# A recurrence and a mixture of experts on one core: first gate parts in pairs, first scores in quarters, last product in halves

## The chip, the core and the metric

The kernel runs on one core of one Trainium2 chip. The metric is the device time of one execution in microseconds (us), median of several runs. Before the change it is 399.98 us (399.85 to 400.6 over 3 runs).

The engines are named as the profile names them: PE is TensorE's matmul row and PEld its weight loads, DVE is VectorE, ACT is ScalarE, POOL is GpSimd, SP is SyncE, whose queue issues most transfers. L583 is line 583 of the kernel before the change.

## The reference

Two parts follow each other. The first is a recurrence over 768 time steps for 4 batches and 8 heads of width 48, with a state of 48 by 48 for each head:

```python
cur = einsum('bhd,bhe->bhde', u * kt, vt)
y[:, :, t] = einsum('bhd,bhde->bhe', rt, state + cur)
state = w * state + einsum('bhd,bhe->bhde', kt, vt)
```

Its output becomes 3072 rows (tokens) of 384. The second part is a mixture of 16 experts in 4 groups of 4. A row picks the group with the largest of 4 group scores, then the expert with the largest of that group's 4 scores; its gate weight is the product of the two softmax values. Then

```python
h = maximum(x[rows] @ w1[expert], 0.0)      # 384 -> 1024
out[rows] = gate * (h @ w2[expert])          # 1024 -> 384
```

All of it is float32.

## The kernel before

**Recurrence.** The 3072 rows are 24 tiles of 128 time steps, four tiles (one for each batch) side by side in time. Within a tile the recurrence is solved in parallel: r is multiplied by powers of the decay w, k by their inverse, and scores k times r for all pairs of time steps are masked to earlier ones. The main loop runs 24 steps `s` (from L860). A step multiplies values with the masked scores of its tile (`values`, L583), prepares scores (`scores`, L536) and masks (`mask`, a predicated copy on VectorE, L543) for tile s+1, or from step `CLOSE` = 5 on for tile s+2, turns k and r of a later tile on TensorE (`turn`, L511; evacuated by ScalarE for k, L520, and by VectorE for r, L522), updates the state (`update`, L594; `carry`, L604 to L608) and adds the state's share of the next tile's output (`state`, L574). GpSimd multiplies r, k and u for the diagonal (`own`, L489 and L490) and scales k (`scaled`, L493); ScalarE and VectorE lay the diagonal into the mask tile `am` (`diagonal`, L561; `diagonal_here`, L554).

**Gates.** The output of a tile leaves PSUM by a ScalarE copy (`values_out`, L612) and is turned into rows (`rows_out`, L630, L634). For the gate scores, four small products for each tile give the parts of a quarter of the columns (`gate_parts`, L619), a ScalarE copy `lT` (L624) takes them out, and a second product adds the quarters (`gate_sum`, L644). In groups of four tiles the routing follows on VectorE (`route_1` to `route_4`), and GpSimd scatters the rows by expert (L230). Steps 3, 4 and 6 do two tiles' gate parts, step 5 one, from step 7 on one for each step. Parts of even tiles below 7 go to the PSUM bank MS, the others to TR. MS also holds the state's update, the gate sums, the prefix and the counts.

**Range flag.** If a decay lies outside a range, the kernel falls back to a slow path. The flag is computed in step 0: `out_of_range` (L752, L753) on VectorE, a product over partitions (`all_out_of_range`, L756) and `in_range` (L759); `go_on` (L762) in step 8. It is used after the experts' counts, by `judge` (L771).

**Start.** Ahead of the loop TensorE does empty transposes of the identity (`turn_nothing`, L422): 13 at first, 2 behind the product that spreads u (L425), and 2 and 4 ahead of the turns of tile 1. The scores of tile 0 are 8 products of 128 by 128 (L530), those of later tiles quarters of 64 wide (L536), each in two passes.

**Experts.** Two experts' first 128 rows are done ahead; then 16 slots follow, slot 1 first and slot 0 last, with row counts as in `SLOTS`. A slot is products up (`up`, L1104), a ReLU on ScalarE (L1109) and products down. Slots 0 and 1 go down with rows on partitions (`rows_down`, L238 to L250): 8 products of 384 columns (L240), a scaling by the gate on ScalarE (L244), and an indirect row write by GpSimd (L245). The other slots go down with columns on partitions (`down`, L1116), from a rearranged copy `w2p` (L1094), and are written by `finish` in blocks (L1128). Weights are fetched three slots ahead by SP (L135, L141).

**Order.** The order on every engine is the order of the calls in the program; semaphores are put in from the tiles' reads and writes, and accesses of two engines to one PSUM bank of a tile are kept apart. One queue's instruction that waits holds all behind it.

Of the kernel before, what the change touches and what calls it, by code (L numbers as in the profile page):

```python
# [9 lines left out]
FP32 = mybir.dt.float32  # L10
I32 = mybir.dt.int32
# [18 lines left out]
def kernel(  # L30
# [52 lines left out]
    def cst(shape, name, dtype=FP32):  # L83
        return const.tile(shape, dtype, name=name)
# [34 lines left out]
    tagA = [cst([P, 2], f"tagA_{i}") for i in range(4)]  # L119
    idA = [cst([P, 1], f"idA_{i}", I32) for i in range(4)]  # L120
    okA = [cst([P, 1], f"okA_{i}", I32) for i in range(4)]
    cnt_s = cst([P, GE], "cnt_s")
# [128 lines left out]

    def tokens(i, n, count):
        nc.vector.memset(idA[i][0:n], NOWHERE)
        nc.vector.tensor_scalar(
            out=tagA[i][0:n, 0:1].bitcast(I32), in0=tagA[i][0:n, 0:1].bitcast(I32), scalar1=2, scalar2=None,
            op0=OP.logical_shift_right,
        )
        nc.vector.tensor_scalar(out=okA[i][0:n], in0=prow[0:n], scalar1=count[0:n], scalar2=None, op0=OP.is_lt)
        nc.vector.copy_predicated(idA[i][0:n], okA[i][0:n], tagA[i][0:n, 0:1].bitcast(I32))

# [13 lines left out]
    with ExitStack() as rec:  # L274
# [3 lines left out]
        rows_ps = YB[:, :, 2 * P : 4 * P]  # L278
        lT_at = (MS[:, 0:P], TR[:, 0, :])

        spare_at = [0]
# [21 lines left out]
        pre_ps = MS[:, 400 : 400 + 4 * GE]  # L303
        cnt_ps = MS[:, 464 : 464 + GE]

        def scratch(shape, i):
# [67 lines left out]

        nc.vector.memset(y_ps, 0.0)
        nc.vector.memset(padded(rp[0]), 0.0)
        nc.vector.memset(padded(rp[NRP - 1]), 0.0)
# [47 lines left out]
        nc.tensor.matmul(u_ps_all, lhsT=ones[0:1, :], rhs=u_row, start=True, stop=True, skip_group_check=True)  # L425
        turn_nothing(2)
        gates_in()
# [96 lines left out]
        def scores(n):  # L524
            kT, rT = rkT.pop((n, "kT")), rkT[n, "rT"]
            for hc in range(HC):
                for e in range(2):
                    rows = slice(DP * e, DP * e + D)
                    if n == 0:
                        nc.tensor.matmul(  # L530
                            PA[:, e, P * hc : P * (hc + 1)], lhsT=kT[rows, hc, :], rhs=rT[rows, hc, :],
                            start=True, stop=True, skip_group_check=True,
                        )
                        continue
                    for z in range(2):
                        nc.tensor.matmul(  # L536
                            PA[64 * z : 64 * (z + 1), e, P * hc + 64 * z : P * (hc + 1)],
                            lhsT=kT[rows, hc, 64 * z : 64 * (z + 1)], rhs=rT[rows, hc, 64 * z : P],
                            start=True, stop=True, skip_group_check=True,
                        )  # L540
# [72 lines left out]

        def gate_parts(n):
            yT = yTs[n]
            lT_ps = lT_at[n % 2 if n < 7 else 1]
            for q in range(NQ):
                e, j = q // 2, q % 2
                nc.tensor.matmul(  # L619
                    lT_ps[32 * q : 32 * (q + 1), :], lhsT=gwp[:, 4 * j + e, :], rhs=yT[:, e, j, :],  # L620
                    start=True, stop=True, skip_group_check=True,
                )
            lT = mid[n] = pool.tile([P, P], FP32, tag="lT", bufs=3, name="lT")
            nc.scalar.copy(lT, lT_ps)  # L624

# [59 lines left out]
        def count(n):  # L685
            nc.tensor.matmul(cnt_ps, lhsT=ones, rhs=cum[:, n, :], start=True, stop=True, skip_group_check=True)

        def keys():
# [62 lines left out]
        def out_of_range():  # L751
            nc.vector.tensor_tensor(out=same, in0=wcol, in1=wraw, op=OP.not_equal)  # L752
            nc.vector.reduce_max(out=same[:, 0:1], in_=same, axis=AX)  # L753

        def all_out_of_range():
            nc.tensor.matmul(cnt_ps[:, 0:1], lhsT=ones, rhs=same[:, 0:1], start=True, stop=True, skip_group_check=True)  # L756

        def in_range():
            nc.vector.tensor_scalar(out=not_ok, in0=cnt_ps[:, 0:1], scalar1=0.5, scalar2=None, op0=OP.is_gt)  # L759

# [66 lines left out]
        scores(0)  # L827
        nc.vector.tensor_mul(WL, pw[:, :, P // 2], pw[:, :, P // 2])
        nc.scalar.copy(wl, WL)
        for t in am[2:4]:  # L830
            nc.scalar.copy(diagonals(t)[:, 0:HERE], spread(nothing.to_broadcast([P, P]), 1, HERE))
        mask(0)
        turn_nothing(2)
        turn(1, "rT")
        turn_nothing(4, TR)
        turn(1, "kT")
# [23 lines left out]
        for s in range(NT):  # L860
# [44 lines left out]
            if s > CLOSE:  # L905
                update(s)
            values_out(s)
            if s == 0:
                own_term(1)
                out_of_range()  # L910
            for n, e, hc in waiting:
                diagonal(n, e, hc, hc + 1)
            waiting.clear()
            if s <= CLOSE:
                scores(s + 1)
                update(s)
                if s == CLOSE:
                    sum_own(s + 3)
                mask(s + 1)
# [5 lines left out]
            if far < NT:  # L925
                turn(far, "kT")
                turn(far, "rT")
            if s == 0:
                all_out_of_range()
                in_range()  # L930
            if whole:
# [7 lines left out]
            for c in range(NB - 1):  # L939
                if s == first(c) + 1:  # L940
                    route_e(c)
            for n in {4: (0, 1), 5: (2, 3), 6: (4,), 7: (5, 6)}.get(s, (s - 1,) if s > 7 else ()):
                gate_sum(n)
            for c in range(NB - 1):
                if s == first(c) + 2:
                    route_p(c)
                    if c == 2:
                        count(12)
            for n in {3: (0, 1), 4: (2, 3), 5: (4,), 6: (5, 6)}.get(s, (s,) if s > 6 else ()):
                gate_parts(n)  # L950
            if s < CLOSE:
                own_term(far)
            for c in range(NB - 1):
# [4 lines left out]
                if s == first(c) + 2:  # L958
                    if c == 2:
                        key = keys()  # L960
                    route_3(c)
                if s == first(c) + (2 if c >= NB - 3 else 3):
# [16 lines left out]
            if s + 1 < NT:  # L979
                state(s + 1)  # L980
            if s == CLOSE - 1:
                turn(s + 3, "kT")
                turn(s + 3, "rT")
                own_term(s + 3)
            if whole:
                diagonal(far, 1)
            if s >= CLOSE and s + 4 < NT:
                sum_own(s + 4)
            if s == 8:
                go_on()  # L990
        for job in late:
# [24 lines left out]
    with ExitStack() as moe:  # L1016
# [55 lines left out]
        def columns(p):  # L1072
# [4 lines left out]
            if s < 2:  # L1077
                tokens(2 + s, SLOTS[s], cnt_s[:, s : s + 1])
                return
# [62 lines left out]
        for p in range(GE):  # L1142
# [10 lines left out]
            if order[p] < 2:  # L1153
                i = order[p]
                po = next_of(downs)
                yt = pool.tile([P, DM], FP32, tag="yd", name="yd")
                rows_down(hTs[p], held(p)[1], 2 + i, SLOTS[i], po, yt)
            else:
                down(p, 0)
# [280 lines left out]
```

## Time and profile before

| | |
|---|---|
| median of 3 runs | 399.98 us (399.85 to 400.6) |
| the profiled execution's own time | 402.09 us |
| its span, first to last instruction | 400.3 us |
| mean granted TensorE clock | 0.998 |
| PE busy in the span | 388.7 us (97%) |
| POOL, ACT, DVE busy | 201.0, 180.4, 153.4 us |
| moved by DMA | 81.80 MB, 204 GB/s over the span |
| recurrence (24 steps) | about 12 to 129 us |
| experts' slots | about 152 to 393 us |

The profile is one execution, about 2 us slower by its own time than the median of the runs; durations are taken from it. The timeline lists runs of alike instructions: start in us, duration, engine, line, operation, tiles (output <- inputs), shape, count, and in brackets the idle time of the engine ahead of it with what seems to have ended it. Ends of matmuls are modelled, so the weight loads (PEld) show better when TensorE goes on. A wait for several things is put down to the one that came last, which is not always the one that held.

### The profile page before, as it was taken

To read this page: it belongs to the slowest core of one execution; us is meant where nothing else is said; L and a number is where in the kernel's file an instruction comes from. 1 tells how busy PE (TensorE), PEld (TensorE's weight loads), DVE (VectorE), ACT (ScalarE), POOL (GpSimd) and SP (SyncE) were. 2 spreads that over 40 slices of the span, in tenths; PEclk is the share of its full clock that TensorE was granted. 3 is DMA by queue.
4 is the path that set the end of the run, shared out by engine and by line. 5 is a ranking of instruction groups with operands and counts; after the bars stand their busy time and mean duration, and the time that the engine had idled before them with its cause. 6 is when DMAs were issued, how large, how long until landed. Compare 5 with 4: busy or idle time off the path is not lost.

```text
span 400.3 us, 10467 instructions
## 1 busy us (share of the span) xinstructions
PE 388.7 (97%) x3963; PEld 361.9 (90%) x3963; DVE 153.4 (38%) x405; ACT 180.4 (45%) x429; POOL 201.0 (50%) x265
## 2 busy tenths in 40 slices
PE   8999999999999999999999999999999999999992
PEld 6787899999888977899999999999999999999981
DVE  7887988888867602101202112111121221211110
ACT  4665888888875211432433424424244244244210
POOL 7999956999842412105162351532624524523542
PEclk9999999999999999999999999999999999999999
DMA  8998999995965977999999999999989999981000
GB/s 159 160 174 159 197 208 221 212 195 147 264 200 123 308 193 212 233 275 258 232 258 243 228 250 266 224 253 284 200 240 259 255 247 268 233 236 28 27 18 27
DMA packets 123118, 81.80 MB, mean 204 GB/s; under 512 B 96863, under 2 KB 114289, under 8 KB 123061
## 3 DMA queue, kind: packets, MB, share of 16 engines
q1 hardware_dynamic: 116019, 71.12, 77.1%
q0 software_dynamic: 4752, 9.55, 8.1%
q8 instruction: 32, 0.52, 0.6%
q10 hardware_dynamic: 2290, 0.40, 0.5%
q14 instruction: 25, 0.20, 0.2%
HBM read 69.89 MB, written 11.67 MB: 204 GB/s over the span
## 4 chain that ended last, share of the span: by engine, by line
issue 46%; PE 29%; POOL 18%; SPq 3%; DVE 2%; DMA 1%; POOLq 1%; ACT 0%
POOL out_dram L1128 16%; PE YB L583 6%; PE PA L536 6%; SPq L323 3%; PE TR L511 3%; PE YB L574 2%; PE YB L630 2%; PE RW L511 2%; PE MS L594 2%; PE TR L619 2%; PE MS L644 1%; DMA vt<-in_v_dram 1%; POOL out_dram L245 1%; PE TR L793 1%; DVE am L543 1%
## 5 line engine op out<-in xcount | busy, mean ns | idle before, releaser
L1128 POOL DMA_INDIRECT out_dram<-yt,idn x93 | 90.4, 972 | 137.1 <-DVE yt L1126 107.0
L1076 DVE STREAM_TRANSPOSE xe<-xg 128x672 f32<-128x672 f32 (+2 forms) x16 | 12.7, 796 | 121.0 <-DMA xg<-x_sorted 88.7
L1116 PE MATMUL YB<-hT,w2p 128*128 128x208 f32 (+10 forms) x336 | 58.7, 328 | 0.0
L1116 PE MATMUL PA<-hT,w2p 128*128 128x208 f32 (+10 forms) x336 | 58.1, 326 | 0.0
L1116 PEld LDWEIGHTS YB<-hT,w2p 128*128 128x128 f32 x336 | 55.8, 190 | 0.0
L1116 PEld LDWEIGHTS PA<-hT,w2p 128*128 128x128 f32 x336 | 55.3, 190 | 0.0
L561 ACT ACTIVATE am<-ident,du 128x128 f32<-128x128 f32 x152 | 50.5, 398 | 0.0
L1125 DVE STREAM_TRANSPOSE yt<-yT 128x672 f32<-128x672 f32 (+1 forms) x14 | 11.8, 842 | 80.4 <-ACT yT L1119 80.4
L1094 ACT COPY w2p<-w 128x1024 f32<-128x1024 f32 x42 | 41.1, 1045 | 3.0 <-DMA w<-in_moe_w_dram 3.0
L543 DVE COPY_PREDICATED am<-later,PA 128x1024 f32<-128x1024 int32 x24 | 31.7, 1323 | 10.8 <-PE PA L536 6.1
L1104 PE MATMUL MS<-xe,w 128*128 128x208 f32 (+12 forms) x192 | 32.8, 320 | 0.0
L1104 PE MATMUL TR<-xe,w 128*128 128x208 f32 (+12 forms) x192 | 32.8, 320 | 0.0
L1104 PE MATMUL RW<-xe,w 128*128 128x208 f32 (+12 forms) x192 | 32.8, 320 | 0.0
L1104 PE MATMUL SB<-xe,w 128*128 128x208 f32 (+12 forms) x192 | 32.7, 320 | 0.0
L1104 PEld LDWEIGHTS SB<-xe,w 128*128 128x128 f32 x192 | 30.8, 190 | 0.6 <-issue 0.2
L1104 PEld LDWEIGHTS MS<-xe,w 128*128 128x128 f32 x192 | 30.7, 190 | 0.0
L1104 PEld LDWEIGHTS RW<-xe,w 128*128 128x128 f32 x192 | 30.7, 190 | 0.0
L1104 PEld LDWEIGHTS TR<-xe,w 128*128 128x128 f32 x192 | 30.7, 190 | 0.0
L230 POOL DMA_INDIRECT x_sorted<-xt,place_i x16 | 16.1, 1003 | 23.6 <-DVE end L719 11.8
L536 PE MATMUL PA<-rT,kT 48*64 48x128 f32 (+1 forms) x736 | 25.6, 255 | 0.5 <-issue 0.5
L583 PE MATMUL YB<-am,vt 128*48 128x128 f32 x384 | 25.9, 277 | 0.1
L490 POOL TENSOR_TENSOR dg<-dg,ub 128x384 f32<-128x384 f32 x24 | 24.1, 1003 | 1.9
(220 smaller groups left out, 560.1 us busy)
## 6 DMA issues: line engine op xcount, KB each, us to landing
w<-in_moe_w_dram SPq DMA_DIRECT2D x128, 384.0 KB, 9.5
vt<-in_v_dram SPq DMA_DIRECT2D x24, 192.0 KB, 4.5
rp<-in_r_dram SPq DMA_DIRECT2D x23, 192.0 KB, 4.3
kt<-in_k_dram SPq DMA_DIRECT2D x22, 192.0 KB, 5.2
xg<-x_sorted SPq DMA_DIRECT2D x36, 85.8 KB, 10.3
x_sorted<-zeros SPq DMA_DIRECT2D x4, 392.0 KB, 4.7
out_dram<-yt,idn POOLq DMA_INDIRECT x93, 7.5
xg<-x_sorted SPq DMA_DIRECT2D x20, 73.5 KB, 8.9
```

The lines of the kernel that those rows point to most:

```text
L230: ins = nc.gpsimd.indirect_dma_start(out=xs_dram, out_offset=bass.IndirectOffsetOnAxis(ap=place_i[:, i : i + 1], axis=0), in_=xt[:, i].rea ...
L490: nc.gpsimd.tensor_mul(dg, dg, ub)
L511: nc.tensor.transpose(ps[:, hc, :], two, ident)
L536: nc.tensor.matmul(PA[64 * z : 64 * (z + 1), e, P * hc + 64 * z : P * (hc + 1)], lhsT=kT[rows, hc, 64 * z : 64 * (z + 1)], rhs=rT[rows, hc ...
L543: nc.vector.copy_predicated(am[n % NAM], later.unsqueeze(1).unsqueeze(1).to_broadcast([P, 2, HC, P]).bitcast(I32), PA.rearrange("p e (h t) ...
L561: nc.scalar.mul(am[n % NAM][:, e, hc, :], ident, dus[n][:, i : i + 1])
L583: nc.tensor.matmul(y_at(e, hc), lhsT=vt[:, n % 2, 2 * hc + e, :], rhs=amn[:, e, hc, :], start=(n < 4 and hc < 2), stop=True, skip_group_ch ...
L1076: nc.vector.transpose(xe[:, :, 0:nb, :], xg[:, 0:nb, 0:QW].rearrange("p i (ko a) -> p ko i a", a=32))
L1094: nc.scalar.copy(o4[:, kk], v4[:, kk])
L1104: nc.tensor.matmul(ph[:, i, 0:n], lhsT=w1[:, ko, P * (f + i) : P * (f + i + 1)], rhs=xe[:, ko].rearrange("p i b -> p (i b)")[:, 0:n], star ...
L1116: nc.tensor.matmul(po[:, 0:n], lhsT=w2p[:, d, fo, :], rhs=hT[:, fo, 0:n], start=(fo == 0), stop=(fo == FO - 1))
L1128: ins = nc.gpsimd.indirect_dma_start(out=out_q, out_offset=bass.IndirectOffsetOnAxis(ap=idn[:, i : i + 1].bitcast(U32), axis=0), in_=yt[:, ...
```

## The change

- **Gate parts.** `gate_parts` takes a list of tiles, writes their parts side by side in TR and takes them out with one copy. Steps 3 and 4 call it, and in step 4 `gate_sum` ahead of it, behind the `state` product of the next tile. In step 5 gate parts come ahead of the sums.
- **Step 4.** The copy `values_out` stands behind the waiting diagonals. The second k turned in step 4 goes to PA in place of TR.
- **First scores.** Tile 0 is done in quarters as the others; a memset clears the unwritten quarter of PA ahead.
- **Start.** The 2, 2 and 4 empty transposes behind the first 13 are gone. The product `WL` and the copy `wl` stand behind the first mask.
- **Range flag.** `out_of_range` moves to the end of step 8 and writes its column into `cum`; the count product of step 14 takes that column too; `in_range` reads it there, `go_on` runs in step 17. The product of step 0 is gone.
- **Last product.** The slot that comes last (slot 0, 96 rows) goes down in two halves of 192 columns, each with its own scaling and row write; row numbers for half rows come from `tokens`.

```diff
+    idH = [cst([P, 1], f"idH_{z}", I32) for z in range(2)]
...
-    def tokens(i, n, count):
+    def half_down(hT, w2, i, n, z, po, yt):
+        cols = slice(DM // 2 * z, DM // 2 * (z + 1))
+        for fo in range(FO):
+            nc.tensor.matmul(
+                po[0:n, 0 : DM // 2], lhsT=hT[:, fo, 0:n], rhs=w2[:, fo, cols], start=(fo == 0), stop=(fo == FO - 1),
+                skip_group_check=True,
+            )
+        nc.scalar.mul(yt[0:n], po[0:n, 0 : DM // 2], tagA[i][0:n, 1:2])
+        ins = nc.gpsimd.indirect_dma_start(
+            out=out.rearrange("n (z w) -> (n z) w", z=2),
+            out_offset=bass.IndirectOffsetOnAxis(ap=idH[z][0:n].bitcast(U32), axis=0),
+            in_=yt[0:n], in_offset=None, bounds_check=2 * N - 1, oob_is_err=False,
+        )
...
+    def tokens(i, n, count, halves=False):
+        tag = tagA[i][0:n, 0:1].bitcast(I32)
+        nc.vector.tensor_scalar(out=okA[i][0:n], in0=prow[0:n], scalar1=count[0:n], scalar2=None, op0=OP.is_lt)
+        if halves:
+            for z in range(2):
+                nc.vector.memset(idH[z][0:n], NOWHERE)
+            nc.vector.tensor_scalar(out=tag, in0=tag, scalar1=1, scalar2=None, op0=OP.logical_shift_right)
+            nc.vector.copy_predicated(idH[0][0:n], okA[i][0:n], tag)
+            nc.vector.tensor_scalar(out=tag, in0=tag, scalar1=1, scalar2=None, op0=OP.bitwise_or)
+            nc.vector.copy_predicated(idH[1][0:n], okA[i][0:n], tag)
+            return
...
-        lT_at = (MS[:, 0:P], TR[:, 0, :])
...
+        lost_ps = MS[:, 464 + GE : 464 + GE + 1]
...
         nc.vector.memset(y_ps, 0.0)
+        nc.vector.memset(PA.rearrange("p e (h z t) -> p e h z t", z=2, t=64)[64:P, :, :, 0, :].rearrange("p e h t -> p (e h) t"), 0.0)
...
         nc.tensor.matmul(u_ps_all, lhsT=ones[0:1, :], rhs=u_row, start=True, stop=True, skip_group_check=True)
-        turn_nothing(2)
...
-                    if n == 0:
-                        nc.tensor.matmul(
-                            PA[:, e, P * hc : P * (hc + 1)], lhsT=kT[rows, hc, :], rhs=rT[rows, hc, :],
-                            start=True, stop=True, skip_group_check=True,
-                        )
-                        continue
...
+        def gate_parts(some):
+            for i, n in enumerate(some):
+                for q in range(NQ):
+                    e, j = q // 2, q % 2
+                    nc.tensor.matmul(
+                        TR[32 * q : 32 * (q + 1), i, :], lhsT=gwp[:, 4 * j + e, :], rhs=yTs[n][:, e, j, :],
+                        start=True, stop=True, skip_group_check=True,
+                    )
+            m = len(some)
+            lT = pool.tile([P, m, P], FP32, tag=f"lT{m}", bufs=3 - m, name="lT")
+            nc.scalar.copy(lT, TR[:, 0:m, :])
+            for i, n in enumerate(some):
+                mid[n] = lT[:, i, :]
...
+        def count_and_range(n):
+            both = cum[:, n : n + 2, :].rearrange("p i e -> p (i e)")[:, 0 : GE + 1]
+            nc.tensor.matmul(
+                MS[:, 464 : 464 + GE + 1], lhsT=ones, rhs=both, start=True, stop=True, skip_group_check=True
+            )
...
-            nc.vector.reduce_max(out=same[:, 0:1], in_=same, axis=AX)
+            nc.vector.reduce_max(out=cum[:, 13, 0:1], in_=same, axis=AX)
...
         scores(0)
-        nc.vector.tensor_mul(WL, pw[:, :, P // 2], pw[:, :, P // 2])
-        nc.scalar.copy(wl, WL)
...
         mask(0)
-        turn_nothing(2)
+        nc.vector.tensor_mul(WL, pw[:, :, P // 2], pw[:, :, P // 2])
+        nc.scalar.copy(wl, WL)
         turn(1, "rT")
-        turn_nothing(4, TR)
         turn(1, "kT")
...
-            values_out(s)
+            if s != CLOSE - 1:
+                values_out(s)
             if s == 0:
                 own_term(1)
-                out_of_range()
             for n, e, hc in waiting:
                 diagonal(n, e, hc, hc + 1)
             waiting.clear()
+            if s == CLOSE - 1:
+                values_out(s)
...
-            if s == 0:
-                all_out_of_range()
-                in_range()
...
+            summed = {4: (0, 1), 5: (2, 3), 6: (4,), 7: (5, 6)}.get(s, (s - 1,) if s > 7 else ())
+            if s > CLOSE:
+                for n in summed:
+                    gate_sum(n)
...
+            parts = {3: (0, 1), 4: (2, 3), 5: (4,), 6: (5, 6)}.get(s, (s,) if s > 6 else ())
+            if s >= CLOSE:
+                gate_parts(parts)
+            if s == CLOSE:
+                for n in summed:
+                    gate_sum(n)
...
                         key = keys()
+                        in_range()
...
                 state(s + 1)
+            if s < CLOSE:
+                for n in summed:
+                    gate_sum(n)
+                if parts:
+                    gate_parts(parts)
             if s == CLOSE - 1:
-                turn(s + 3, "kT")
+                turn(s + 3, "kT", PA[:, 0].rearrange("p (h t) -> p h t", t=P))
...
             if s == 8:
+                out_of_range()
+            if s == 17:
                 go_on()
...
+                if p == last:
+                    for z in range(2):
+                        yt = pool.tile([P, DM // 2], FP32, tag="yh", name="yh")
+                        half_down(hTs[p], held(p)[1], 2 + i, SLOTS[i], z, next_of(downs), yt)
```

## The prediction

> **What bounds the kernel now.** I read the page's first part, then the busy time by stretches, then the timeline of the engines where a stretch falls short. The page's engine line:
>
> ```profile
> PE 388.7 (97%) x3963; PEld 361.9 (90%) x3963; DVE 153.4 (38%) x405; ACT 180.4 (45%) x429; POOL 201.0 (50%) x265
> ```
>
> TensorE is the bound, yet 97% is an average. The table of stretches (length, then busy us of PE, PEld, DVE, ACT, POOL with counts, clock, DMA share, GB/s):
>
> ```profile
> 30.00:40.00 10.00, 9.47 (x188) 7.69 (x190) 7.07 (x12) 5.01 (x15) 9.46 (x16) 1.00 0.85 159
> ...
> 200.00:300.00 100.00, 100.00 (x591) 100.00 (x590) 17.47 (x36) 35.05 (x61) 42.10 (x44) 1.00 1.03 244
> ```
>
> The stretch from 10 to 20 us has 9.23 of 10. From 50 us on TensorE has no hole worth naming, so what is won before stays won, unless a transfer is late. Before 45 us it waits, and the change works exactly there. The weight-load row of the timeline, a line for each run of matmuls, shows the holes of steps 0, 3, 4 and 5 (the bracket is the idle time ahead):
>
> ```profile
> 12.14 0.83 PEld L583 LDWEIGHTS YB<-am,vt 128*48 128x48 f32 x16 [0.30 <-DVE am L543]
> ...
> 16.54 0.30 PEld L756 LDWEIGHTS MS<-same,ones 128*128 128x128 f32 x2 [0.83 <-DVE R L604]
> ...
> 28.36 0.47 PEld L511 LDWEIGHTS RW<-ident,rp 128*128 128x128 f32 x4
> 29.31 0.19 PEld L619 LDWEIGHTS MS<-yT,gwp 128*32 128x32 f32 x8 [0.48 <-issue]
> ...
> 34.81 0.52 PEld L644 LDWEIGHTS MS<-sel,lT 128*128 128x128 f32 x4 [0.48 <-POOL zeros L880]
> ...
> 36.81 0.42 PEld L511 LDWEIGHTS TR<-ident,kp 128*128 128x128 f32 x4 [0.48 <-POOL dg L490]
> ...
> 42.09 0.52 PEld L644 LDWEIGHTS MS<-sel,lT 128*128 128x128 f32 x4 [0.43 <-DVE ts L607]
> ```
>
> The POOL names are not the cause: those tiles are unrelated. What ends at these moments is VectorE reading the bank MS (R L604 until 29.24, ts L607 until 34.70 and 42.04) and ScalarE's second lT copy out of TR (until 36.70). Step 0 on VectorE:
>
> ```profile
> 10.51 0.34 DVE L828 TENSOR_TENSOR SB<-pw 128x4 f32<-128x4 f32 x1
> 10.76 1.32 DVE L543 COPY_PREDICATED am<-later,PA 128x1024 f32<-128x1024 int32 x1
> ...
> 14.33 0.49 DVE L752 TENSOR_TENSOR same<-wcol,wraw 128x4 f32<-128x4 f32 x1
> ...
> 14.93 1.32 DVE L543 COPY_PREDICATED am<-later,PA 128x1024 f32<-128x1024 int32 x1
> ```
>
> Both value products (L583) wait for a mask (L543), and small VectorE work stands ahead of each mask. The tail, in the timeline's last two lines:
>
> ```profile
> 393.18 0.58 ACT L244 ACTIVATE yd<-YB,tagA 96x384 f32<-96x384 f32 x1 [4.83 <-PE YB L240]
> 394.03 0.94 POOL L245 DMA_INDIRECT out_dram<-yd,idA  x1 [1.76 <-ACTq L1170]
> ```
>
> [...]gate sums into their own columns of MS wait for L607. [...]here each costs 0.17 to 0.20 us ("issue" ahead of L583, L574, L536). [...]Here transposes take 421 ns until about 9 us and 272 ns after.
>
> **The change part by part**, against the profiled execution (span 400.3, its own time 402.09).
>
> *Step 0.* (a) Two empty transposes go: the next loads move from 6.23 to 5.96, −0.27, on the chain turn, rT (DVE 7.61), kT (8.40), scores (9.20). r had landed at 4.6, so nothing else holds it. The other six removed transposes stood in TensorE's wait for the mask: 0. (b) Scores in 32 records of quarters instead of 16: L536 takes 1.03 from its start to the next run, L530 took 1.12; they must only be done when the mask may start. Bounds: +1.0 if run at half clock, −0.09. The new memset of PA (like the 0.48 one of YB) falls into VectorE's 0.58 idle ahead of L381; bare, it would cost 0.48. (c) The WL product (0.34) leaves the place ahead of mask(0). That then waits for ScalarE's diagonals, which end at 10.61 − 0.27 = 10.34: start 10.38 instead of 10.76, and values(0) at 11.76, −0.38. The wl copy now waits behind the mask, until 12.05, and kT(1)'s copy behind it ends near 12.8 as before, so scores(1) gain only 0.25; yT(0)'s copy gains 0.39 and ScalarE's diagonals for tile 1 end at 14.4 instead of 14.76. (d) Range flag: L752 and L753 (0.65) leave the place ahead of mask(1), which now waits for those diagonals: 14.45 instead of 14.93, end 15.78. (e) The L756 product, which waited for R until 16.49 and held TensorE's queue with values(1) behind it, goes: values(1) start at 15.83 instead of 16.86. **Step 0: −1.03**; bounds −0.35 (quarters cold) and −1.3.
>
> POOL's products run back to back from 9.81 to 42; they start 0.27 earlier with T2. Tile 3's k product ends at 17.5, its turn comes at 18.7; tile 8's at 37.3 against 38.2. They cover the shift.
>
> *Step 3.* Before: turn done 28.80, gate parts 29.31, state 29.91, values 30.50. After, with mode changes of 0.18 to 0.20 and the rows' own 0.40 each: 28.80 + 0.20 + 0.40 (state) + 0.18 + 0.40 (parts) + 0.18 = 30.16. **−0.34.** TR is free then (kT copy ends 29.31). Bounds −0.1, −0.45.
>
> *Step 4.* Before: turn done 34.30, values(5) 37.84. After: 0.20, state 0.40, 0.18, sums 0.55, parts 0.38, 0.18, kT 0.39 (into PA, so no wait for lT), rT 0.44, 0.20: 37.22. **−0.62**; one mode change more is in it. Bounds −0.4, −0.85. The yT(4) copy goes behind three diagonals (0.98), which find du(5) ready and ScalarE idle for 1.32: at most 0.4 late; its first user is step 5. mask(5) may start when the scores end (32.6), not at 33.13.
>
> *Step 5.* Parts go ahead of the sums, into the wait for L607: parts at 41.85 (kT copy leaves TR at 41.78), sums 42.10 to 42.62, scores near 42.82 instead of 43.00. **−0.2**; bounds 0, −0.35. One lT copy of 256 columns (a 128x256 ACT copy: 0.41) replaces two of 0.27; the pair's single buffer is free because its two sums are issued first.
>
> *Step 8, 14, 17.* L752 and L753 now stand ahead of L607 in step 8 (go_on, 0.13, leaves): ts ends at 62.15 instead of 61.65, the next gate sum comes at 62.36, mask(11) near 64.9 is needed at 69.78. 0; bare 0.5. One more column in the count product (L686, 16 columns, 0.35 busy): 0.
>
> *Last product.* 16 products of 384 columns become 32 of 192; 0.32 per 384 either way, +0.05 at most 0.3. ScalarE's last scaling is 0.58 for 384; by the slope of L1109 (0.33 at 192, 0.52 at 416) 192 columns less save 0.16. POOL: six row writes 1.28 apart end at 392.27, the first half's at 393.54, the second starts at 393.85, as ScalarE allows: −0.16. The last transfer moved 147 KB between 395.5 and 396.45; half of it saves about 0.45. [...]**−0.6**; bounds +0.3, −1.0. The extra descriptor-issuing instruction hides behind the product.
>
> Moved steps issue no DMA; SP's queue is passed by none. Sum: 1.03 + 0.34 + 0.62 + 0.20 + 0.60 = 2.79. Span 400.3 to 397.5; on the median 399.98, which lies 2.1 below the profiled execution, **397.2**. The bounds add to −0.5 and −3.9.
>
> **Rivals.** *Start shortened (398.2):* the quarters run at half clock and mask(0) waits for them, or a buffer order costs step 4 its gain. For: the clock rises near 9.2, where the scores now start. Against: ScalarE's diagonals hold the mask until 10.34 anyway. Step 0 then gives 0.35, the tail less: −1.8.
>
> *Gain lost to the weights (399.4):* DMA shares of 1.03 in the expert stage; an earlier TensorE would then wait for weights and only the tail counts. Against: ScalarE's w2p copy waits for weights 3.0 us in all; the latest, 177.0 to 180.0, is needed at 188.3, and weights are asked for by steps that move along.
>
> *Slower (401.5):* without eight transposes the array stays at half clock. The price is up to 4 us for a step (TensorE issues 4.06 of every 4.06 us in steps 1 and 2). It decides from about three quarters of a cold step past step 0. [...]against: [...]between 10.1 and 15.8 TensorE has 4.3 us of work (two pairs of turns at 0.88, values 1.01, scores 1.03, update 0.49).
>
> *Larger (396.2):* every bound at its good end.
>
> **Numbers.** Likeliest 0.53 (its own range 396.4 to 398.0), shortened start 0.23, lost 0.12, slower 0.07, larger 0.05. The range reaches over the first two and into the lost case: 396.0 to 399.5. A change of 0.2% (0.8 us) is about what a measurement can tell. Faster: 0.53 + 0.23 + 0.05 and a little of the lost case, 0.82; same 0.11; slower 0.07.
>
> **What would show it.** Step 0: mask(0) near 10.4, mask(1) near 14.45, values(1) near 15.8. Steps 3 to 5: no wait over 0.3 ahead of L644, or of L511 into PA; values(5) near 35.85 (37.84 less 1.99), step 6 on at the old pace. Tail: scaling of 0.42, last landing near 3.1 us after its issue, was 3.6. Wrong if: transposes of 421 ns after 10 us, PEld waits on DMA after 150, or L644 waiting for L607 in step 9.

## The result, and the profile after

The changed kernel is slower: 403.36 us (median of 22 runs, 400.65 to 404.89) against 400.62 for the kernel before on the same chips (22 runs), a ratio of 1.0062, 95% interval 1.0043 to 1.008. Forecast was 397.2. Ratios in this document leave out executions more than 1.5% above the fastest of their kernel and medians do not, so a ratio can differ from the quotient of two medians. The profiled execution has a span of 401.5 us and a time of its own of 403.36; its mean granted clock is 0.993 (0.998 before). Lines are those of the changed kernel: `values` is L599 (was L583), `scores` L552 (L536), `mask` L559 (L543), `turn` L533 (L511), `gate_parts` L634 (L619), `gate_sum` L662 (L644), `own` L511 and L512 (L489, L490), `scaled` L515 (L493).

The page's engine line says little: TensorE's busy time is the same within 0.3 us.

```profile
PE 389.0 (97%) x3985; PEld 364.7 (91%) x3985; DVE 154.1 (38%) x409; ACT 180.9 (45%) x427; POOL 202.1 (50%) x266
```

The busy time by stretches (PE, PEld, DVE, ACT, POOL, clock, DMA share, GB/s) says where to look:

```profile
30.00:40.00 10.00, 9.00 (x182) 7.28 (x176) 6.64 (x10) 5.56 (x17) 8.27 (x14) 1.00 1.03 177
40.00:50.00 10.00, 8.82 (x134) 7.67 (x134) 7.47 (x17) 5.78 (x17) 9.47 (x15) 0.83 1.17 199
200.00:300.00 100.00, 100.00 (x591) 100.00 (x590) 17.46 (x36) 35.41 (x61) 42.28 (x44) 1.00 0.99 242
```

From 30 to 40 us TensorE is busy for less time than before (9.47), and from 40 to 50 us, where before had 9.81 of 10 at full clock, it has 8.82 at a clock of 0.83. DMA shares are higher: 1.03 against 0.85 from 30 to 40 us. The weight loads of TensorE, at the places that the prediction showed:

```profile
12.18 0.83 PEld L599 LDWEIGHTS YB<-am,vt 128*48 128x48 f32 x16 [0.74 <-DVE am L559]
...
16.24 0.82 PEld L599 LDWEIGHTS YB<-am,vt 128*48 128x48 f32 x16 [0.67 <-DVE am L559]
...
29.02 0.38 PEld L634 LDWEIGHTS TR<-yT,gwp 128*32 128x32 f32 x16 [0.18 <-issue]
...
34.17 0.52 PEld L662 LDWEIGHTS MS<-sel,lT 128*128 128x128 f32 x4 [0.18 <-POOL sel L440]
...
35.77 0.42 PEld L533 LDWEIGHTS PA<-ident,kp 128*128 128x128 f32 x4 [0.68 <-POOL kp L515]
...
41.17 0.71 PEld L533 LDWEIGHTS TR<-ident,kp 128*128 128x128 f32 x4 [1.89 <-POOL kp L515]
```

The holes that the change was to close are closed: gate parts and sums stand 0.18 us behind the products ahead of them, within the 0.17 to 0.20 us of "issue" that the prediction counts for each mode change. But the turn of tile 7 waits 0.68 us and that of tile 8 waits 1.89 us, both for GpSimd's scaled k; and after the second wait the weight loads of the turn take 0.71 us for four instead of 0.42: the clock is down (0.50 from 42 to 44 us). GpSimd, which ran without a gap from 9.81 us on before, shows why it is late:

```profile
31.18 1.00 POOL L511 TENSOR_TENSOR dg<-rp,kt 128x384 f32<-128x384 f32 x1 [3.23 <-DMA rp<-in_r_dram]
...
40.12 1.00 POOL L515 TENSOR_TENSOR kp<-kt,T 128x384 f32<-128x384 f32 x1
```

GpSimd stood for 3.23 us until a load of r had landed, and the product of tile 8 ends at 41.1 us. Before, the same two products were these; tile 8 was ready at 37.6 us, and TensorE came to its turn at 40.37:

```profile
27.63 1.02 POOL L489 TENSOR_TENSOR dg<-rp,kt 128x384 f32<-128x384 f32 x1
...
36.59 1.00 POOL L493 TENSOR_TENSOR kp<-kt,T 128x384 f32<-128x384 f32 x1
```

Most of the delay was there before the load was asked for. SP issues one load after another, and at the pair of loads that this one opens it was 3.2 us behind; here before the change, then after it:

```profile
22.54 3.01 SPq L323 DMA_DIRECT2D rp<-in_r_dram  x2
```

```profile
25.71 1.91 SPq L345 DMA_DIRECT2D rp<-in_r_dram  x2
```

The masks on VectorE:

```profile
10.77 1.36 DVE L559 COPY_PREDICATED am<-later,PA 128x1024 f32<-128x1024 int32 x1 [0.48 <-PE PA L552]
...
14.83 1.36 DVE L559 COPY_PREDICATED am<-later,PA 128x1024 f32<-128x1024 int32 x1 [0.33 <-PE MS L610]
```

The first mask waits for the scores, which ran mostly at half pace: TensorE takes 1.83 us for them, from 8.81 on, where those of tile 1 take 1.10. It is the pace of the start: before the change, runs of four transposes begin 0.85 us apart up to 8.15 and 0.44 apart from 10.61 on. The trace's records of the granted clock begin at 9.14 us there and at 10.37 in the changed kernel, at 1.00. Below, cold means this pace. The tail:

```profile
394.92 0.42 ACT L260 ACTIVATE yh<-PA,tagA 96x192 f32<-96x192 f32 x1 [2.18 <-PE PA L256]
395.61 0.92 POOL L261 DMA_INDIRECT out_dram<-yh,idH  x1 [0.40 <-ACTq L1206]
```

At the first values of step 8 TensorE is 2.06 us behind (57.01 against 54.95). In the expert stage it waits once, 1.2 us, for `xe`.

### The profile page after: what moved, and what is told of

It is laid out like the page before. It is cut to its first block, busy times and chain, and to the rows that moved or that the text cites. A ratio compares the mean times of both kernels' runs of the same rounds, so it can differ in the third digit from the quotient of the medians.

```text
span 401.5 us, 10503 instructions
## 1 busy us (share of the span) xinstructions
PE 389.0 (97%) x3985; PEld 364.7 (91%) x3985; DVE 154.1 (38%) x409; ACT 180.9 (45%) x427; POOL 202.1 (50%) x266
## 4 chain that ended last, share of the span: by engine, by line
issue 46%; PE 24%; POOL 21%; SPq 3%; DMA 3%; DVE 1%; POOLq 1%
POOL out_dram L1160 16%; PE YB L599 5%; PE PA L552 4%; SPq L345 3%; DMA rp<-in_r_dram 3%; PE TR L533 2%; PE YB L590 2%; PE YB L648 2%; PE RW L533 2%; PE TR L634 2%; PE MS L610 1%; POOL dg L511 1%; POOL dg L512 1%; PE MS L662 1%; POOL out_dram L246 1%
## 5 line engine op out<-in xcount | busy, mean ns | idle before, releaser
L1126 ACT COPY w2p<-w 128x1024 f32<-128x1024 f32 x42 | 41.1, 1043 | 14.6 <-DMA w<-in_moe_w_dram 14.5
L559 DVE COPY_PREDICATED am<-later,PA 128x1024 f32<-128x1024 int32 x24 | 32.5, 1354 | 9.7 <-PE PA L552 6.2
L552 PE MATMUL PA<-rT,kT 48*64 48x64 f32 (+1 forms) x768 | 27.1, 260 | 0.0
L599 PE MATMUL YB<-am,vt 128*48 128x128 f32 x384 | 25.9, 277 | 1.0 <-DVE am L559 0.9
L552 PEld LDWEIGHTS PA<-rT,kT 48*64 48x64 f32 x768 | 21.3, 136 | 4.7 <-issue 4.1
```

The lines of the kernel that those rows point to most:

```text
L552: nc.tensor.matmul(PA[64 * z : 64 * (z + 1), e, P * hc + 64 * z : P * (hc + 1)], lhsT=kT[rows, hc, 64 * z : 64 * (z + 1)], rhs=rT[rows, hc ...
L559: nc.vector.copy_predicated(am[n % NAM], later.unsqueeze(1).unsqueeze(1).to_broadcast([P, 2, HC, P]).bitcast(I32), PA.rearrange("p e (h t) ...
L599: nc.tensor.matmul(y_at(e, hc), lhsT=vt[:, n % 2, 2 * hc + e, :], rhs=amn[:, e, hc, :], start=(n < 4 and hc < 2), stop=True, skip_group_ch ...
L1126: nc.scalar.copy(o4[:, kk], v4[:, kk])
```

## The experiments

### Parts alone, and the queue's share

The first theory was that TensorE, freed of its early waits, overtakes the loads, and that the hole then lets the clock fall. Rivals: the array is colder without the empty transposes, or the profiled execution was unlucky. The changed kernel ran once more, and each part alone on the kernel before.

> The changed kernel once more, for a second trace and more times. Loads theory (TensorE, freed of its early waits, arrives at the key turn of tile 8 before GpSimd has made its product, because a load of r came late; it then idles near 40 us and the array falls to half clock): times spread over 400.6 to 405, granted clock between 0.98 and 1.00, and the trace either shows GpSimd waiting over 1 us for an r load before 32 us together with a half-clock stretch near 42 us, or neither. Clock theory (the array is less warm because eight empty transposes are gone): a half-clock stretch in every execution, at the same place. Chance theory (the profiled execution was unlucky): ratio below 1.002.

> Only the start of the change: no eight empty transposes, first scores in quarters, the WL product after mask(0), range flag counted with tile 12. Steps 3 to 5 and the last product as before. Loads theory: values(1) about 0.6 us earlier, as in the changed kernel, and no hole near 40 us: 399.6 to 400.8 (0 to -0.6 against before). Clock theory: this part carries the loss, 402 to 403, with a half-clock stretch as in the changed kernel.

> Only the gate parts in pairs behind the state products in steps 3 and 4 (and step 5's order); start and last product as before. Loads theory: values(5) about 1.0 us earlier than before, the turn of tile 8 waits for GpSimd's product by under 1 us, clock 0.99 to 1.00, 399.5 to 401.5. Clock theory: no loss here, the full gain of 1 us, 399.4 to 399.8. Weights theory (what is won early is lost to waits on weights or gathered columns after 150 us): no gain, 400.2 to 400.8.

> Only the last product in two halves with two row writes. All theories: from the start of the last product to the end about 0.5 us less than before (GpSimd's last start about 6.17 after the product's start instead of 6.30, landing 3.1 to 3.3 us later instead of 3.6), 399.9 to 400.3, granted clock as before.

The times tell nothing: the kernel before took 408 to 425 us beside them (median 417.61), and in the four traces TensorE stands for 1 to 2 us at a time with nothing to wait for that the profile shows. Medians were 423.46, 417.9, 419.61 and 423.64; ratios for the three parts, 0.9988, 0.9851 and 1.012, rest on 3 to 6 executions beside 5. The first 60 us of the traces are readable, and they held what no theory had foreseen. Here is the hardware queue's line for the first 100 us (packets, MB, share of 16 engines), before the change:

```profile
q1 hardware_dynamic: 74301, 16.05, 82.2%
```

and in the changed kernel:

```profile
q1 hardware_dynamic: 74171, 15.58, 92.4%
```

About as many packets take 92.4% of the engines' time instead of 82.2%. In the four runs the share was 92.5% for the changed kernel, 85.0% for the start alone, 83.4% for steps 3 to 5 alone, and 91.8% for the *halves* alone, which in these 100 us issue the same instructions as the kernel before. The hole ahead of the turn of tile 8 came back in the changed kernel (1.89 us again, this time without a fall of the clock, which is 1.00 from 40 to 50 us). So the loads are slow in the kernels that hold the last product's halves, in every trace: not luck, and not the clock.

What these kernels share from the first microsecond on is memory. The halves need two index columns, `idH`, in the list of constants. Each takes 32 bytes of every partition here, and all that is laid out later moves by 64: the tiles that r is loaded into begin at byte 127,808 of a partition before (64 past a multiple of 256), at 127,872 (128 past) after. A row of r is 192 bytes, and rows stand 256 apart. At 64 a row lies within one block of 256 bytes, at 128 it lies across two. That a row across two takes longer was the author's guess; the packet records in the next section bear on it.

### The places in SBUF

> The changed kernel with its two new index columns put into the unused part of an old constant (idA_2, which the last product no longer uses), so that no later tile moves by 64 bytes in SBUF. Places theory (the two new constants push the r tiles from 64 to 128 bytes past a multiple of 256, and their 192-byte rows then cross such a multiple and transfer more slowly): the DMA queue's share of the first 100 us falls from 92.4% to 82 to 85%, as before the change; GpSimd waits for no r load by more than 0.7 us before 32 us, no half-clock stretch near 42 us, and the time is 397 to 398.5 where before is 400.6. Chance theory and clock theory (slow loads or a cold array that the places don't touch): as the changed kernel, 401 to 404.

```diff
-    idA = [cst([P, 1], f"idA_{i}", I32) for i in range(4)]
-    idH = [cst([P, 1], f"idH_{z}", I32) for z in range(2)]
+    idA = [cst([P, 2 if i == 2 else 1], f"idA_{i}", I32) for i in range(4)]
+    idH = [idA[2][:, z : z + 1] for z in range(2)]
```

> The kernel before with two unused constants in the same place, nothing else: all later tiles move by 64 bytes. Places theory: DMA share of the first 100 us 91 to 93% (82.2% before), r loads land in about 4.9 us instead of 4.3, GpSimd waits for r loads between 20 and 32 us; slower than before by 0.5 to 3 us. Other theories: same time within 0.2%, share 82 to 85%.

```diff
+    unused = [cst([P, 1], f"unused_{z}", I32) for z in range(2)]
```

> The changed kernel with four more unused constants, so that the r tiles stand at 0 bytes past a multiple of 256 (before: 64; changed kernel: 128). If crossing a multiple of 256 is what slows the rows, they cross none here: DMA share of the first 100 us 82 to 85%, 397 to 398.5. If any move away from the old place is at fault, or the added constants themselves: 91 to 93%, 401 to 404.

The same line with `range(4)`, added to the changed kernel.

> The kernel before with the last product halved and nothing moved in SBUF. All theories that keep the places apart from the halves: DMA share 82 to 85%, 0.4 to 0.7 us less than before (about 400.0 where before is 400.6), all of it after the last product starts.

The halves on the kernel before, with `idH` laid out as in the first of these.

| kernel | r tiles past 256 | queue share, 0 to 100 us | 192-byte packets, mean | median, us | ratio to before (401.03 us) |
|---|---|---|---|---|---|
| before, two constants more | 128 | 90.8% | 18.7 ns | 404.86 | 1.0071 (1.0047 to 1.0096) |
| changed, nothing moved | 64 | 84.7% | 16.2 ns | 400.62 | 0.9977 (0.9953 to 1.0) |
| changed, moved by 192 | 0 | 83.2% | 16.2 ns | 399.5 | 0.9965 (0.9938 to 0.9991) |
| before, halves, nothing moved | 64 | 83.4% | 16.4 ns | 401.0 | 1.0003 (0.9983 to 1.0023) |

Two unused constants make the kernel before 0.7% slower. Four more unused constants make the changed kernel *faster*, so it is not that constants were added, nor that the tiles moved, but where they stop. The shares of the queue came as expected, within a point; the times of the two changed kernels did not reach the 397 to 398.5 that had been expected. In the packet records of 14 traces, the 73,728 packets of 192 bytes take 18.7 to 19.1 ns on average where r stands at 128, and 16.2 to 16.6 where it stands at 64 or 0. Before the change 68,517 of them took 16 ns or less, after it 51,970.

All tiles behind the constants moved together, so what is shown is that their place costs time, and not that it is r's rows. Two things speak against r's rows as the whole cause. Rows of k and v lie without gaps, and in every version three of four cross a multiple of 256 (their tiles begin 224 bytes past one before, 32 after); before the change most of them are as quick as r. And the records of SP's queue, counted off in the order in which the packets start, 1,024 to a load, show slow stretches and not slow rows. In the changed kernel the first load, of r at 128, has a mean of 15.7 ns (17.3 before). The next eleven, of r, k and v alike, have 21.6 to 27.7 (15.0 to 19.1 before). The load of r that follows has 15.4 again. That a crossing row takes longer does not account for this. What in the new place makes the loads slow together stays open.

With the places kept, the early part of the forecast stands. TensorE's weight loads in the changed kernel without the shift:

```profile
33.51 0.52 PEld L662 LDWEIGHTS MS<-sel,lT 128*128 128x128 f32 x4 [0.18 <-issue]
...
34.63 0.42 PEld L533 LDWEIGHTS PA<-ident,kp 128*128 128x128 f32 x4 [0.20 <-POOL zeros L899]
...
35.66 0.82 PEld L599 LDWEIGHTS YB<-am,vt 128*48 128x48 f32 x16 [0.17 <-issue]
...
42.02 0.83 PEld L599 LDWEIGHTS YB<-am,vt 128*48 128x48 f32 x16 [0.18 <-DMA x_sorted<-zeros]
```

No hole, and step 6 begins at 42.02 (at 42.00 in the version moved by 192) instead of 44.46 in the kernel before:

```profile
44.46 0.82 PEld L583 LDWEIGHTS YB<-am,vt 128*48 128x48 f32 x16 [0.18 <-issue]
```

GpSimd waits for r by 0.20 us, not 3.23, and has tile 8 ready at 37.5:

```profile
27.47 1.01 POOL L511 TENSOR_TENSOR dg<-rp,kt 128x384 f32<-128x384 f32 x1 [0.20 <-DMA rp<-in_r_dram]
...
36.45 1.01 POOL L515 TENSOR_TENSOR kp<-kt,T 128x384 f32<-128x384 f32 x1
```

In the kernel before with two constants more TensorE is only 0.7 us late at step 6 (45.15 against 44.46), and of these 0.65 stand at the first values already (12.79 against 12.14): GpSimd's slack covers the slower loads. The lateness is handed on in SP's queue instead. Three pieces of the second early expert's weights are asked for from 129.2 us on, where before it was 123.9, and TensorE waits for weights at that expert:

```profile
138.28 2.92 PE L794 MATMUL PA<-xeA,w 128*128 128x128 f32 x24 [2.47 <-DMA w<-in_moe_w_dram]
```

### Where the rest of the gain went

Without the shift TensorE is 2.5 us early when the first early expert begins (125.18 us, against 127.73 in the kernel before with halves), yet by the ratios only 0.9 us arrives at the end, 1.4 in the version moved by 192. In that one's trace there is a wait at the second early expert:

```profile
134.36 4.54 PE L815 MATMUL PA<-xeA,w 128*128 128x128 f32 x24 [2.13 <-DMA w<-in_moe_w_dram]
```

2.13 us of waiting, and then 4.54 us for 24 products that take 2.92 elsewhere: the clock had fallen (a mean of 0.97 from 100 to 150 us, where the version with nothing moved has 1.00). The version with nothing moved was profiled in an execution of 405.67 us, well above its median. It has no wait for weights at the second early expert (132.10 us), and what its expert stage shows is the bad end: 5.8 us of waits for gathered rows in all (the changed kernel had 1.2), the longest here:

```profile
357.73 3.50 PE L1136 MATMUL SB<-xe,w 128*128 128x172 f32 x12 [3.57 <-DVE xe L1108]
```

Two remedies were tried on it, each on the kernel before too. SP's queue stood 6.3 us for the sorted rows at step 21 with three pieces of the second early expert's weights behind it; the first remedy asks for these in steps 18 to 20.

```diff
-            some = 1 if s == NT - 8 else 2 if s < NT - 1 else 3
+            some = 1 if s == NT - 8 else 3 if NT - 7 < s < NT - 3 else 2 if s < NT - 1 else 3
```

> The changed kernel with nothing moved in SBUF, and with three pieces of the second early expert's first weights asked for in steps 18, 19 and 20 instead of 21 to 23, so that they stand ahead of the gathered rows in SyncE's queue (that queue stood still for 6.3 to 6.7 us waiting for the sorted rows, with these pieces behind it). Weights theory (the early gain of 2.5 us is partly lost because weights and gathered rows land late once TensorE is early): no wait for w ahead of the second early expert's up product, most executions at 397 to 398.5, median 1.5 to 2.5 us under before. If the loss is elsewhere: as without this (399.5 to 400.6 where before is 401.0, a gain of 0.4 to 1.5).

> The kernel before with the same three pieces asked for earlier. Weights theory: TensorE of the kernel before reaches the up product late enough, so little is won: 0 to -0.8. If the pieces' place matters by itself, as much as in the changed kernel: -1 or more.

> Only the start of the change (steps 3 to 5 and last product as before, nothing moved in SBUF). Values of step 8 start about 1.2 us earlier than in the kernel before (54.95); of that 0.3 to 1.2 reach the end.

> Only the moves in steps 3 to 5 (nothing moved in SBUF). Values of step 8 start 1.0 to 1.6 us earlier than before; of that 0.3 to 1.3 reach the end.

Inconclusive: the kernel before took 418.8 to 437.4 us beside them (median 429.68), and the four had medians of 429.59, 434.16, 429.35 and 433.04. They ran once more.

> The changed kernel with nothing moved in SBUF and three weight pieces asked for earlier, once more[...]. Weights theory: no wait for w ahead of the second early expert's up product, most executions at 397 to 398.5 and the median 1.5 to 2.5 us under before. Otherwise a gain of 0.4 to 1.5, as without the early pieces.

> The kernel before with the three pieces asked for earlier, once more. Weights theory: 0 to -0.8 against before. If the pieces' place matters by itself: -1 or more.

> Only the start of the change, nothing moved in SBUF, once more. The trace gave values of step 8 at 53.8 instead of 54.95; 0.3 to 1.2 of it reach the end: ratio 0.997 to 0.9993.

> Only the moves in steps 3 to 5, nothing moved in SBUF, once more. Values of step 8 about 1.3 us earlier than before; 0.3 to 1.3 of it reach the end: ratio 0.9968 to 0.9993.

| kernel | median, us | ratio to before (401.11 us) |
|---|---|---|
| changed, nothing moved, weights early | 398.97 | 0.9955 (0.9934 to 0.9976) |
| before, weights early | 402.7 | 1.0029 (1.0007 to 1.0051) |
| start alone | 399.4 | 0.9958 (0.9937 to 0.9979) |
| steps 3 to 5 alone | 400.1 | 0.9977 (0.9959 to 0.9996) |

The start alone brings 1.7 us and steps 3 to 5 alone 0.9, more than the start was expected to bring and within what the steps were. The start's own trace doesn't show its 1.7: the values of step 8 come at 55.33 us there, behind a cold start, where before it was 54.95. Together the two would be 2.6, about what the trace with nothing moved shows at step 8 (52.52, 2.4 early); the kernel that has both, and the halves, gains less than the sum. With early weights the 24 products at the second early expert start without a wait (134.38 us), which says little, since they did so at 132.10 without the remedy; and their trace, again of a long execution (408.69 us), has 5.1 us of waits for `xe`. Waits of this size stand in these two long executions alone. The second remedy gives the gathered rows a fourth buffer and asks for them ahead of the weights:

```diff
-            xg = xgs[p] = pool.tile([P, 8, QX], FP32, tag="xg", bufs=3, name="xg")
+            xg = xgs[p] = pool.tile([P, 8, QX], FP32, tag="xg", bufs=4, name="xg")
...
-            if 0 < p and p + 2 < GE:
-                fetch_rows(p + 2)
+            if p + 3 < GE:
+                fetch_rows(p + 3)
```

> The changed kernel with nothing moved in SBUF, and with each later expert's gathered rows asked for ahead of its weights instead of behind the weights of the next (a fourth buffer for the rows). In the profiled execution without this TensorE waited 5.8 us in the expert stage for xe, whose rows land about 12 us after they are asked for, behind 3 MB of weights. If it is the place of the rows in the queue that gives back the early gain: no wait for xe, most executions 397 to 398.5, median 2 to 2.8 us under before. If the transfers as a whole are too slow, the wait moves to the weights: ratio as without this, 0.995 to 0.999.

> The kernel before with the same order of rows and weights. Its TensorE had no wait for xe in the profiled execution: 0 to -0.8, with fewer executions above 401 if those come from late rows.

Measured: 399.4 us, ratio 0.996 (0.9934 to 0.9986) to before (400.68), less than the 2 to 2.8 us expected, and 401.53, ratio 1.0015 (0.9997 to 1.0034), for the kernel before with the same edit. The waits for `xe` are gone from TensorE, and its profiled execution has a span of 396.9 us, with one wait on a transfer left:

```profile
133.74 2.92 PE L814 MATMUL PA<-xeA,w 128*128 128x128 f32 x24 [1.08 <-DMA w<-in_moe_w_dram]
```

Neither remedy helps the kernel before, and the changed kernel with nothing moved and either of them is faster than the kernel before (by 1.8 and 1.6 us). But 0.9955 and 0.996 can't be told from the 0.9977 without a remedy, and executions with the rows first still spread from 396.96 to 403.35 us. That late weights and rows take back part of what TensorE wins is seen in single traces; that they take the whole difference, or that the remedies cure it, is not shown.

## Why the prediction was wrong

**The step that failed: the cost of the last product.** Its sum counts products, scalings, row writes and the transfer, and counts the two index columns at nothing, without naming them. Their 64 bytes are the loss: put into the kernel before they cost 0.7%, and without them the changed kernel's ratio is 0.9977 instead of 1.0062. That is about 3.4 of the 5.3 us between the forecast (2.8 faster) and the measurement (2.5 slower). The other 1.9 are missing with nothing moved too, where 0.9 of the 2.8 us arrive. The sentence "Moved steps issue no DMA; SP's queue is passed by none" is true, and overlooks that moving the tiles can make the loads slower.

**"They cover the shift"**, said of POOL's products, rested on loads as quick as before: tile 8's k ready at 37.3 against a turn at 38.2. With nothing moved this came out, 37.5 and 38.19. In the changed kernel the load that GpSimd waited for was asked for 3.2 us later, loads into r's tiles took 4.9 us to land at the median instead of 4.3, and GpSimd, one product of 1.0 us behind another, could not make it up.

**"What is won before stays won, unless a transfer is late."** The reservation counted. With nothing moved 2.4 us are won at step 8 and 0.9 arrive. The rival that gave the gain to the weights (0.12) is what single traces show: 2.13 us for weights in the version moved by 192, 1.2 for gathered rows in the changed kernel. Whether such waits are all of the missing 1.9 us stays open. The argument against that rival was the 3.0 us for which ScalarE's rearranging copy waited in all; in the changed kernel it waits 14.5, though TensorE doesn't wait for it there.

**The slower rival** had its place and price wrong. It put a half clock at the start, for want of empty transposes. A long cold start does occur: in one of the ten traces without them, of the start alone, the array was cold until 15.5 us and values(1) came at 17.57; in none of the ten with them was it cold for so long, which doesn't show that they warm it. That 4.3 us of work between 10.1 and 15.8 us speak against a cold array was the author's estimate: in that trace TensorE's timeline shows no wait in these 5.7 us, and the array was cold nearly throughout. But in the changed kernel's trace the fall came at 41 us, after a hole made by a late load. From values(5) to values(6) the changed kernel took 9.73 us against 6.37 without the shift: of these 3.36 the hole is 1.89, and three runs of transposes at half clock (0.50 granted) are 1.09 (0.71, 0.87 and 0.87 of weight loads instead of 0.42, 0.47 and 0.47).

**Steps 0 and 3 to 5** were right, to a few hundredths where the forecast was a count of rows. Starts and intervals in us, before and in the changed kernel with nothing moved:

| | forecast | before | without the shift | measured |
|---|---|---|---|---|
| step 0: mask(0) start | -0.38 | 10.76 | 10.22 | -0.54 |
| step 0: mask(1) start | -0.48 | 14.93 | 14.25 | -0.68 |
| step 0: values(1) start | -1.03 | 16.86 | 15.63 | -1.23 |
| step 3: values(3) to values(4) | -0.34 | 5.49 | 5.15 | -0.34 |
| step 4: values(4) to values(5) | -0.62 | 7.34 | 6.73 | -0.61 |
| step 5: values(5) to values(6) | -0.20 | 6.62 | 6.37 | -0.25 |

The gains of step 0 vary with the execution: values(1) starts at 15.61 to 16.30 us in nine traces with the changed start and at 17.57 in the cold one, at 16.41 to 17.39 in the ten with the old start. In the changed kernel itself step 3 shows its 5.15 too. Of the bounds in step 0, "quarters run at half clock" happened in its trace (1.83 us for the scores): mask(0) at 10.77 gained nothing, and yet values(1) came 0.62 earlier, from parts (d) and (e).

**The tail** was right in kind and too large. GpSimd's last write starts 6.17 us after the last product does, instead of 6.30 (forecast -0.16, measured -0.13), the scaling takes 0.42. From there to the end it is 5.65 to 5.90 us in six traces with halves and 5.69 to 6.27 in six without (means 5.77 and 6.03; those beside which the kernel before took about 401 us), so the smaller transfer saves some 0.25, not 0.45, and on the time the halves alone show nothing: 1.0003, with room for 0.7 us.

**The base.** The profiled execution of before held two stalls of TensorE in the middle of groups, 0.75 us at 103 and 0.89 at 110, that no wait explains, though the prediction saw no hole worth naming from 50 us on. Compared with it the changed kernel loses little in the traces; the runs show more.

## What to carry to other kernels

Adding a small tile can move every tile behind it, here by 64 bytes for two: before an edit that allocates is costed at nothing, look which tiles it moves, and compare the queue's share for the same packets in both traces (92.4% against 82.2% here). One run of the old kernel with only the allocation added, as here, tells the price (0.7%). When a kernel's producers live on slack that a loaded DMA queue provides, a step saved on the consumer spends that slack, and a hole may cost more than its length (here 1.89 us, and 1.09 more in the transposes behind it). Part of what is saved ahead of a stage with many transfers can come back there as a wait (2.13 us for weights in the version moved by 192).

## What the runs showed of the hardware

- Where the tiles laid out behind the constants lie sets the price of the same loads: their 73,728 packets of 192 bytes take 16.2 to 16.6 ns as a mean with r's tiles at 64 or 0 past a multiple of 256, and 18.7 to 19.1 at 128. The slow packets come in stretches, in loads of r, k and v alike; r's rows at 128 can be quick (15.7 and 15.4 ns for two loads).
- TensorE's clock fell after some holes of about 2 us and not after others. At the turn of tile 8 it fell to 0.50 after 1.89 us in one trace of the changed kernel and stayed at 1.00 in the other after the same 1.89. At the second early expert it fell after 2.13 us (move by 192; 24 products in 4.54 us, a mean clock of 0.97 from 100 to 150 us) and not after 2.47 (the kernel before with two constants more; 2.92 us, 1.00).
- When the array warms at the start differs between executions of kernels with the same start. In the trace of the start alone it was cold until past 14.5 us (tile 1's scores take 1.55 us there, where 1.10 is the warm value), though TensorE's timeline shows no wait from 7.73 us to past 16: it stayed cold through about 7 us of work. In another trace of the same kernel it was cold until about 10. The scores of tiles 0 and 1 in the first of these:

```profile
8.81 1.98 PE L531 MATMUL PA<-rT,kT 48*64 48x128 f32 x32
...
14.50 1.55 PE L531 MATMUL PA<-rT,kT 48*64 48x128 f32 x32
```

Kernels with all empty transposes vary as well: their values(0) start between 11.69 and 12.79 us.
